# Another recorded order for an attention and two gated layers, with fillers placed by transfers at 1.1 of the model

## The chip, the cores and the metric

The kernel runs on one core of one Trainium2 chip, with TensorE (PE), VectorE (DVE), ScalarE (ACT), GpSimd (POOL) and the transfer queue of SyncE (SP). The metric is the device time of one execution in microseconds; lower is better.

## The reference

Three layers follow each other, for a batch of 4, sequences of 576, 8 heads of 64 and a width of 512. The attention sees a window of 128 positions with a bias by distance; the second layer has a width of 1024 inside.

```
scores = scale * q @ k^T                       # B, H, S, S
scores = where(0 <= rel < 128, scores - slope * rel, -1e9)
x = softmax(scores) @ v                        # laid out as B, S, 512
h = relu(x @ w_in)                             # 512 -> 1024
x = (h * sigmoid(conv3(h))) @ w_out            # 1024 -> 512
x = (sigmoid(conv5(x)) * (x @ w_val)) @ w_out2 # 512 -> 512
```

## The kernel before

Each batch is cut into two halves of the sequence, eight units in all. For a unit the kernel does the attention (`attention` for the first batch, `duo` for the later ones), then `hidden` (w_in, relu, a convolution of 3 taps, the gate), `mixed` (w_out, a convolution of 5 taps), `valued` (w_val times the gate) and `output`. float32 products are made of two rounded halves each: a product of two tiles is three matmuls (L965, L966, L967, or all three at L959 in the later, half-width form). The weights come as float32 in blocks of 128 x 512 into three buffers raw0 to raw2; `widen` (L468 the transfer, L469 and L480 on DVE, L471 on ACT, then a rounding on ACT or POOL, L486 or L487, and a subtraction on POOL, L448) splits each.

In the attention of the first batch a group of blocks passes these steps: scores (PE, L741), the bias and the row's minimum (DVE, L690), the exponential (ACT, L695), the turned-over sum (POOL L699, DVE L701), the scaling (POOL L756, ACT L758 or DVE L762), transposes (PE, L768), an eviction (ACT, L423) and the product with v (PV; PE, L795). Scores and transposes lie in the banks pss0 to pss2, PV in psx0, the dense products in pm0 to pm3. A bank is free for the next product only when the last reader of the one before is done; in `hidden` that is the third multiply-add at L430.

Nothing sets the order at run time. The functions only record operations, with a number each, what they read and write, and the engines that they could run on. `ORDER` is a list of 2,731 entries, a number with a letter: P for PE, A for ACT, D for DVE, G for POOL, S for SP. `Program.order` walks this list, gives each operation that engine, and counts a start for each from a table of durations. Each engine then gets its instructions in the order of the list, and the starts that were counted are used for one more thing: fillers. A filler (L1178) is a small matmul on constants without a use for its result, and the loop at the end of the kernel puts as many as fit into a counted gap of PE:

```
                if fill and o.start < FILL:
                    warm(max(pe, until), o.start)
```

Until 80 us of counted time (`FILL`), a gap gets one for each 160 ns near the start and one for each 125 ns later. `XFER` is a factor on the counted time of each transfer (L160 and after):

```
            if e == "SP":
                dma = max(dma, t + 1100.0) + o.xfer * XFER
                o.end = dma + LAND + o.lat
```

where `o.xfer` is 1.33 times what the recording function gives, 2.85 ns for each of 512 columns for a weight block. So both the list and `XFER` decide how many fillers stand where; the list alone decides the rest.

Of the kernel before, what the change touches and what calls it, by code (L numbers as in the profile page):

```python
# [29 lines left out]
0D 2G 5G 10G 19S 21P 1S 11G 13G 6G 135S 8S 48S 139S 33P 77S 22D 23D 3G 4G 9G 24A 25A 26G 14G 7G 20S 34D 35D 37A 50P  # L30
51D 27D 30G 36A 38G 136D 145S 28A 29P 31P 137A 52D 54A 138D 151S 49S 39D 42D 32A 62P 40G 41P 53A 140D 141A 55G 56D 57G
15G 59A 106S 43P 44A 142D 143G 63D 64D 58P 60P 61A 65A 66A 79P 80D 91P 459S 144G 81D 83A 67G 82A 84G 92D 93D 157S 147A
68D 69G 146D 95A 94A 45P 46A 943D 85D 71G 70P 72P 73A 148D 163S 153A 86G 87P 47D 88G 96G 89P 90A 149G 152D 74P 78S 97D
98A 100G 154D 155A 169S 150G 944D 156G 108P 109D 107S 945D 120P 497S 111A 75A 121D 110D 99P 101P 102A 461P 122D 112A
113G 76D 123A 114D 305P 124A 462D 16G 117G 158D 115A 116P 118P 159A 125G 126D 295P 463D 129G 127G 119A 473P 160D 161G
175S 465A 464A 164D 165A 474D 128P 130P 466G 946D 103P 162G 131A 485P 476A 467D 470G 166D 181S 167G 168G 285P 475D
104A 105D 468A 486D 171A 469P 471P 472A 170D 132P 947D 172D 187S 499P 487A 488G 133A 134D 306P 477A 478G 173A 489D
500D 490G 17G 535S 479D 480G 501D 286P 177A 176D 948D 503A 307A 491P 287A 18G 174G 482G 308A 178D 193S 179G 288A 309D
289D 296P 297A 182D 12G 502A 183A 504G 180G 290D 298A 184D 199S 498S 481P 483P 484A 511P 291A 299D 492A 292D 189A 523P
573S 310D 185G 186G 293A 300D 311A 512D 301A 315P 316P 524D 514A 294G 312D 302D 525A 526G 513D 313A 188D 317A 303G  # L40
336P 337P 515A 314G 505D 190D 205S 319A 326P 327P 506A 516G 338D 195A 508G 507P 509P 194D 304G 318A 320G 527D 528G
517D 339A 196D 211S 520A 340D 328A 191G 529P 510A 537P 321D 460S 341D 329A 200D 322A 323D 518G 342A 530A 192G 519P
330D 201A 343D 324A 331D 197G 202D 217S 521P 522A 344A 325G 332A 538D 203A 206D 198G 207A 346P 347P 539D 541A 348A
333D 561P 549P 550D 807S 356P 204G 208D 540A 212D 349D 209A 223S 562D 494G 542G 543D 213A 210G 357P 358A 563A 546G
551D 350D 359A 493P 536S 367P 368P 214D 229S 334A 360A 351D 345G 495A 218D 219A 361G 564G 496D 215A 220D 235S 335G
352A 544A 553A 216G 552A 554G 531P 574S 949D 224D 545P 547P 225A 532G 353D 381P 362D 548A 575P 221G 555D 558G 226D
241S 363A 950D 222G 354A 355G 556A 557P 559P 227A 228G 565D 364D 230D 231A 382P 395P 560A 952D 576D 232D 247S 566A
587P 951D 533A 365A 577D 236D 233A 567P 366G 588D 237A 534D 234G 589D 568A 578A 579A 238D 253S 383P 242D 243A 239G
240G 369P 599P 1604D 590A 244D 259S 370P 373A 375A 384P 600D 248D 372A 371A 569P 396P 397P 398P 249A 810S 809S 374D
591A 376G 377D 245G 580G 570G 246G 250D 386A 389A 387A 592G 378D 265S 251A 388D 379D 581D 601A 602G 409P 410P 385A  # L50
254D 390G 603D 604G 605P 593D 255A 256D 400A 582A 583P 401A 403A 252G 391D 811S 808S 271S 812S 411P 412P 260D 261A
404G 402D 392D 594A 595P 596A 597P 262D 277S 584A 571A 257G 585P 606A 263G 598A 393D 423P 572D 266D 258G 586A 607P
805S 806S 814S 414A 405D 267A 416D 424P 406D 264G 415A 268D 399A 417A 418G 413A 380A 407D 428P 429P 608G 272D 273A
425D 438P 269A 270G 419D 426A 427G 274D 609A 394A 420D 421D 439P 791S 275A 276G 610D 422A 279A 433P 430D 431A 278D
# [12 lines left out]
705D 1163S 921D 925A 926G 715D 915S 706D 912D 726P 727A 731A 927D 930A 928A 720D 729D 732G 934A 721D 739P 740P 741P
932A 936S 916S 929D 733A 734G 933D 728A 753P 742A 744A 746A 931D 935D 953P 937S 1166S 730D 758P 735D 954D 955P 736D
763P 959D 956D 743A 748A 745D 960D 759P 747G 749G 750D 957D 764P 958G 970G 971D 737A 722A 964A 754P 965D 975G 765D
707A 755D 967A 756A 760D 751D 761G 766G 1192P 1195D 1193D 938P 939A 1197A 757D 762D 941A 767G 1194D 940D 768P 769P  # L70
1199A 752A 942D 976A 781P 1198A 1196D 770D 977D 1171P 1174D 968D 1175D 1167S 1200A 1201G 973A 771A 987G 772G 773P
1178A 1179A 785P 1220S 1172D 1173D 1177A 974D 777P 774P 1176A 1180G 1202D 1209A 984G 778P 1181D 1182A 1184A 775D 988P
989P 1205D 981D 1203D 1188A 1189D 1207A 1211S 1208D 779A 998P 1186A 1221S 1210D 1187D 1206D 978G 990A 786P 991A 1204D
992D 782P 787A 1018P 993D 994A 982G 979G 980D 985A 999P 983D 783A 1019P 986D 1212S 780S 776S 1168G 1169G 1000A 1001A
1008P 1452S 1473S 1183D 995D 1020A 1022A 1002D 1229P 1185D 1003D 1021A 1023G 1009P 1232D 1004A 1230D 1236A 1190S 1472S
1191S 1005D 1029P 1233D 1454S 788S 1170G 1024D 1010A 1011A 1039P 1231D 1025A 1012D 1234A 1030P 1031A 1026D 996G 997G
1013D 1014A 1040P 1453D 1456S 1059P 1060P 1032A 1015D 1049P 1041A 1027G 1028G 1033D 1034D 1006A 784S 1042A 1237A 1043D
1044D 1235A 1007G 1035A 1036D 1468S 1470S 1224S 1223S 1222S 1225S 1238G 1045A 1061A 1217G 1214G 1213P 1215A 1218D
# [101 lines left out]
class Program:  # L180
# [29 lines left out]
    def order(self):  # L210
# [1043 lines left out]
```

## Time and profile before

| | |
|---|---|
| median of 3 runs | 394.82 us (394.79 to 396.17) |
| the profiled execution | 396.73 us, span 394.9 us |
| PE busy | 383.7 us (97%) |
| DVE, ACT, POOL busy | 345.3, 296.0, 241.8 us |
| fillers | 74 |

The span runs from the first to the last instruction. PE is busy nearly throughout, so the table is read as the work of PE and the few places where it has none; the others are busy for 61% to 87% of the span.

### The profile page before, as it was taken

What the parts mean: (1) busy time and instruction counts of PE and PEld (TensorE: products, weight loads), DVE (VectorE), ACT (ScalarE), POOL (GpSimd) and SP (SyncE); (2) the same over time, 40 slices, a digit from 0 to 9 for tenths busy, and PEclk for the clock granted to TensorE, in tenths of its full rate; (3) what the DMA queues carried; (4) which work ended last, traced back from release to release, by engine and by line L of the source; (5) the groups of instructions that cost most, each with busy time, mean ns of one, the idle gap of its engine ahead of it and who ended that gap; (6) DMA issues with size and microseconds to landing.
All of it is one profiled execution on the core that took longest, in us unless ns stands there. A gap on an engine that the chain in (4) does not pass through costs nothing.

```text
span 394.9 us, 10880 instructions
## 1 busy us (share of the span) xinstructions
PE 383.7 (97%) x3878; PEld 335.0 (85%) x3878; DVE 345.3 (87%) x1045; ACT 296.0 (75%) x902; POOL 241.8 (61%) x378
## 2 busy tenths in 40 slices
PE   8899999999999999999999999999999999999996
PEld 7578888899999878998899866799888876898886
DVE  3899999999899999988998999988999898957782
ACT  4889999968796888638887979757986768824561
POOL 2768999958876577825757668460663344741640
PEclk9899999999999999999999999999999999999999
DMA  7967777744646096372762654826455260131001
GB/s 238 314 228 273 239 261 259 238 132 123 170 94 135 11 212 209 71 186 56 185 130 50 195 106 144 165 94 206 106 88 93 77 150 0 26 75 52 0 2 54
DMA packets 64918, 53.77 MB, mean 136 GB/s; under 512 B 44512, under 2 KB 57184, under 8 KB 64864
## 3 DMA queue, kind: packets, MB, share of 16 engines
q1 hardware_dynamic: 64864, 53.08, 49.8%
q8 instruction: 30, 0.49, 0.5%
q14 instruction: 24, 0.20, 0.1%
HBM read 38.51 MB, written 4.72 MB: 109 GB/s over the span
## 4 chain that ended last, share of the span: by engine, by line
PE 53%; DVE 9%; ACT 3%; issue 1%; POOL 0%; DVEq 0%; ACTq 0%
PE pm L959 27%; PE pm L965 7%; PE pm L966 7%; PE pm L967 6%; PE pss L879 3%; PE pss L940 2%; DVE gts L430 2%; DVE t L430 1%; DVE pp L912 1%; DVE hout L610 1%; DVE g L447 1%; DVE gts L1084 1%; ACT pss L695 1%; DVE pss L690 1%; ACT g L1053 0%
## 5 line engine op out<-in xcount | busy, mean ns | idle before, releaser
L959 PE MATMUL pm<-xh,hin 128*128 128x320 f16 (+1 forms) x504 | 68.6, 286 | 0.1
L959 PEld LDWEIGHTS <-hin 128*128 128x128 f16 x504 | 48.0, 97 | 14.2 <-issue 1.1
L959 PEld LDWEIGHTS <-hout 128*128 128x128 f16 x384 | 37.0, 97 | 11.0 <-issue 1.7
L441 POOL TENSOR_TENSOR gts<-gts,t 128x317 f32<-128x317 f32 (+3 forms) x36 | 29.3, 813 | 27.8 <-ACT t L440 11.2
L965 PE MATMUL pm<-g,wout 128*128 128x254 f32 (+3 forms) x128 | 39.7, 310 | 0.3 <-DVE st L701 0.3
L965 PE MATMUL pm<-g,wval 128*128 128x318 f32 (+3 forms) x128 | 39.8, 311 | 0.2
L965 PE MATMUL pm<-g,wo 128*128 128x318 f32 (+3 forms) x128 | 39.2, 306 | 0.0
L690 DVE CUSTOM_DVE_ANT_0 pss<-pss,bm 128x192 f32<-128x192 f32 (+2 forms) x90 | 30.9, 348 | 9.2 <-PE pss L741 7.8
L966 PE MATMUL pm<-g,wo 128*128 128x318 f32 (+3 forms) x128 | 38.1, 298 | 0.3 <-DVE g L447 0.3
L966 PE MATMUL pm<-g,wout 128*128 128x254 f32 (+3 forms) x128 | 38.0, 297 | 0.0
L966 PE MATMUL pm<-g,wval 128*128 128x318 f32 (+3 forms) x128 | 38.0, 297 | 0.0
L967 PE MATMUL pm<-g,wout 128*128 128x254 f32 (+3 forms) x128 | 37.8, 296 | 0.1
L967 PE MATMUL pm<-g,wval 128*128 128x318 f32 (+3 forms) x128 | 37.7, 295 | 0.0
L967 PE MATMUL pm<-g,wo 128*128 128x318 f32 (+3 forms) x128 | 37.7, 294 | 0.0
L1016 ACT ACTIVATE t<-t 128x318 f32<-128x318 f32 (+3 forms) x64 | 28.3, 447 | 10.7 <-DVE t L430 10.1
L695 ACT ACTIVATE pss<-pss,st 128x192 f32<-128x192 f32 (+2 forms) x81 | 30.2, 373 | 6.6 <-DVE st L690 4.8
L430 DVE SCALAR_TENSOR_TENSOR t<-pm,cc,t 128x254 f32<-128x254 f32 (+7 forms) x56 | 28.0, 513 | 2.1 <-ACT t L423 1.2
L430 DVE SCALAR_TENSOR_TENSOR t<-pm,wcc,t 128x318 f32<-128x318 f32 (+3 forms) x56 | 28.2, 512 | 1.3 <-POOL t L441 0.4
L430 DVE SCALAR_TENSOR_TENSOR t<-t,pm 128x318 f32<-128x318 f32 (+3 forms) x64 | 28.4, 448 | 0.9 <-ACT t L1016 0.6
L912 DVE SCALAR_TENSOR_TENSOR pp<-pss,st,pp 128x192 f16<-128x192 f32 (+2 forms) x79 | 28.1, 385 | 1.0 <-ACT pp L908 0.7
L959 PE MATMUL pm<-ghin,hout 128*128 128x318 f16 x192 | 26.8, 298 | 0.2 <-DVE t L430 0.2
L699 POOL TENSOR_SCALAR st<-st 128x4 f32<-128x4 f32 (+3 forms) x44 | 8.8, 199 | 29.6 <-ACT pss L695 11.4
(200 smaller groups left out, 1305.6 us busy)
## 6 DMA issues: line engine op xcount, KB each, us to landing
raw<-in_w_out SPq DMA_DIRECT2D x12, 512.0 KB, 4.0
raw<-in_w_in SPq DMA_DIRECT2D x8, 512.0 KB, 5.1
qkt<-in_qk SPq DMA_DIRECT2D x10, 384.0 KB, 4.5
vr<-in_vN SPq DMA_DIRECT2D x36, 96.0 KB, 3.1
qkt<-in_qk SPq DMA_DIRECT2D x6, 480.0 KB, 4.5
pp<-in_qk SPq DMA_DIRECT2D x6, 480.0 KB, 4.4
raw<-in_vN SPq DMA_DIRECT2D x6, 384.0 KB, 3.8
pp<-in_qk SPq DMA_DIRECT2D x6, 384.0 KB, 3.6
```

Source lines behind the costliest of these rows:

```text
L430: pg.add("DVE", dve_t(n, 0 if isinstance(scalar, float) else 1), lambda: nc.vector.scalar_tensor_tensor(out=out, in0=in0, scalar=scalar, i ...
L441: pg.add("POOL", pool_t(n, True), lambda: nc.gpsimd.tensor_tensor(out=out, in0=out, in1=t, op=ALU.add), prio, (tk,), (key,))
L690: pg.add("DVE", 75 + 1.05 * nkey, lambda: nc.vector.tensor_tensor_reduce(out=s, in0=s, in1=tab[:, 192 - nkey:192], op0=ALU.add, op1=ALU.mi ...
L695: pg.add("ACT", act_t(nkey, True, 2), lambda: nc.scalar.activation(out=to, in_=s, func=AF.Exp, scale=-1.0, bias=best, accum_out=total), pr ...
L699: pg.add("POOL", 165, lambda: nc.gpsimd.tensor_scalar(ri, total, 1e-9, norm, op0=ALU.add, op1=ALU.mult), pr, reads, writes, port=True)
L879: m.append(nc.tensor.matmul(out=s[64 * x:64 * x + 64], lhsT=q_t[y][i][64 * h:64 * h + 64, 64 * h:64 * h + 64], rhs=k_t[y][64 * h:64 * h + ...
L912: pg.add("DVE", dve_t(nkey, 1), lambda sc=sc, hi=hi, lo=lo, ri=ri: nc.vector.scalar_tensor_tensor(out=lo, in0=sc, scalar=ri, in1=hi, op0=A ...
L959: return [nc.tensor.matmul(out=o, lhsT=a, rhs=b_, start=first and i == 0, stop=last and i == 2) for i, (a, b_) in enumerate(((wh, hi), (wh ...
L965: return [nc.tensor.matmul(out=o, lhsT=wh, rhs=hi, start=first, stop=False), nc.tensor.matmul(out=o, lhsT=wh, rhs=lo, start=False, stop=Fa ...
L966: nc.tensor.matmul(out=o, lhsT=wh, rhs=lo, start=False, stop=False),
L967: nc.tensor.matmul(out=o, lhsT=wl, rhs=hi, start=False, stop=last)]
L1016: pg.add("ACT", act_t(Ng), lambda c=c: nc.scalar.activation(out=c, in_=c, func=AF.Tanh, scale=0.5), pr, (), (ak,))
```

## The change

The list is another one: every entry from the first row on may stand elsewhere, and some operations that more than one engine can do have another letter. `XFER` is 1.1 instead of 0.93. Nothing else differs.

```
 ORDER = """
-0D 2G 5G 10G 19S 21P 1S 11G 13G 6G 135S 8S 48S 139S 33P 77S 22D 23D 3G 4G 9G 24A 25A 26G 14G 7G 20S 34D 35D 37A 50P
...
+0D 19S 21P 1S 5G 6G 7G 2G 3G 4G 135S 48S 8S 139S 20S 22D 23D 33P 77S 25A 24A 34D 145S 49S 50P 26G 35D 37A 36A 137A 27D
...
-XFER = 0.93
+XFER = 1.1
```

What the list does is seen in the order of instructions. First TensorE, at the start, in the attention of the first half batch: L741 is a score, L768 a transpose, L795 a PV product (one line further down in the new kernel: L742, L769, L796); L1178 and L1179 are fillers. The old order:

```order
L768 MATMUL pss2_199<-eye_110,pp_192 128x128 x2
...
L741 MATMUL pss1_198<-qkt_177 128x64
L741 MATMUL pss1_198<-qkt_177 128x128
L741 MATMUL pss2_199<-qkt_177 128x192 x2
L795 MATMUL psx0_200<-pp_192,vr_178 64x256 x2
L795 MATMUL psx0_200<-pp_192,vr_178 64x128 x2
L768 MATMUL pss0_197<-eye_110,pp_192 128x128 x4
L768 MATMUL pss1_198<-eye_110,pp_192 128x128 x2
L795 MATMUL psx0_200<-pp_192,v16_179 64x256 x2
L795 MATMUL psx0_200<-pp_192,v16_179 64x128 x2
L741 MATMUL pss0_197<-qkt_177 128x64
L741 MATMUL pss0_197<-qkt_177 128x128
```

One filler stands ahead of these rows and one at the dots. In the new order:

```order
L742 MATMUL pss1_198<-qkt_177 128x128
L769 MATMUL pss2_199<-eye_110,pp_192 128x128
L796 MATMUL psx0_200<-pp_192,vr_178 64x256 x2
L796 MATMUL psx0_200<-pp_192,vr_178 64x128 x2
L742 MATMUL pss2_199<-qkt_177 128x192 x2
L769 MATMUL pss0_197<-eye_110,pp_192 128x128 x4
L742 MATMUL pss0_197<-qkt_177 128x64
L742 MATMUL pss0_197<-qkt_177 128x128
L796 MATMUL psx0_200<-pp_192,v16_179 64x256 x2
L796 MATMUL psx0_200<-pp_192,v16_179 64x128 x2
L769 MATMUL pss1_198<-eye_110,pp_192 128x128 x2
```

The scores on pss2 have moved behind the first PV product, and those on pss0 ahead of the second. Ahead of these rows stand eight fillers, a transpose and two fillers more.

The second place is on VectorE, in the hidden layer of the first half batch, around the last multiply-add on the bank pm1. The old order:

```order
L430 SCALAR_TENSOR_TENSOR t2_134<-pm2_195,cc_109,t2_134 128x254
L430 SCALAR_TENSOR_TENSOR t1_133<-pm1_194,cc_109,t1_133 128x254
L690 ISA pss0_197,st1_191<-pss0_197,bm_113 128x192
L690 ISA st1_191 128x1
L690 ISA pss1_198,st1_191<-pss1_198,bm_113 128x192
...
L430 SCALAR_TENSOR_TENSOR t2_134<-t2_134,pm2_195 128x254
L430 SCALAR_TENSOR_TENSOR t1_133<-t1_133,pm1_194 128x254
```

In the new order the last multiply-add on pm2 is done two rows before the first of these:

```order
L481 SCALAR_TENSOR_TENSOR gts_141<-pm3_196,raw0_114 128x512
L431 SCALAR_TENSOR_TENSOR t1_133<-pm1_194,cc_109,t1_133 128x253
L702 RECIPROCAL st1_191<-st1_191 128x1
L691 ISA pss0_197,st1_191<-pss0_197,bm_113 128x192
L691 ISA st1_191 128x1
L431 SCALAR_TENSOR_TENSOR t1_133<-pm1_194,cc_109,t1_133 128x254
L425 TENSOR_SCALAR t3_135<-pm0_193,cc_109 128x254
L691 ISA pss0_197,st1_191<-pss0_197,bm_113 128x192
L691 ISA st1_191 128x1
L470 TENSOR_SCALAR raw1_115,acc_111<-raw1_115 128x512
L431 SCALAR_TENSOR_TENSOR t1_133<-t1_133,pm1_194 128x254
```

The last one on pm1 has moved behind two steps of the widening of weights (L470, L481), two minima and a first tap on pm0.

Over the whole program TensorE gets 109 fillers instead of 74: 55 instead of 40 up to the products of the fourth PV, and 54 instead of 34 from there to the middle of the first w_out products. DVE has 1,015 instructions instead of 1,022, ACT 762 instead of 760 and POOL 388 instead of 383.

## Rows read from the trace of the kernel before

**Rows 1.** The page's first part: busy time, share, instructions.

```profile
PE 383.7 (97%) x3878; PEld 335.0 (85%) x3878; DVE 345.3 (87%) x1045; ACT 296.0 (75%) x902; POOL 241.8 (61%) x378
```

**Rows 2.** Busy time of each engine by stretch.

```profile
core 0: us, PE busy (x) PEld busy (x) DVE busy (x) ACT busy (x) POOL busy (x), PEclk, DMA share, GB/s
0.00:12.00 12.00, 9.69 (x61) 8.38 (x61) 4.95 (x26) 5.98 (x20) 3.89 (x23) 1.00 0.76 253
12.00:16.00 4.00, 2.88 (x20) 1.95 (x20) 3.32 (x16) 3.50 (x16) 2.87 (x7) 1.00 0.87 263
16.00:20.00 4.00, 3.85 (x18) 2.68 (x17) 2.99 (x10) 2.50 (x6) 3.83 (x7) 0.60 0.95 349
20.00:24.00 4.00, 3.31 (x24) 3.05 (x24) 3.09 (x15) 3.59 (x13) 1.36 (x5) 0.97 0.84 263
24.00:60.00 36.00, 34.22 (x291) 30.39 (x290) 35.25 (x120) 35.23 (x103) 33.97 (x56) 1.00 0.73 251
60.00:380.00 320.00, 318.16 (x3381) 277.50 (x3379) 288.83 (x846) 241.21 (x738) 193.96 (x281) 1.00 0.47 118
380.00:395.00 15.00, 11.63 (x92) 10.99 (x90) 6.90 (x18) 3.97 (x11) 1.89 (x3) 1.00 0.10 35
```

**Rows 3.** The fillers, by their tile: ns least/median/most, first and last start.

```profile
L1178 PE MATMUL psx<-one x74: 245/246/368, 1.1 to 55.5; 128*128 128x192 bf16 x74
```

**Rows 4.** PE's timeline up to 40 us: start, duration, what, wait.

```profile
11.21 0.25 PE L1178 MATMUL psx<-one 128*128 128x192 bf16 x1
...
11.51 0.25 PE L1178 MATMUL psx<-one 128*128 128x192 bf16 x1
...
16.88 1.54 PE L795 MATMUL psx<-pp,v 128*64 128x256 f32 x8
18.36 2.25 PE L741 MATMUL pss<-qkt 128*128 128x64 f32 x8
...
22.35 0.41 PE L965 MATMUL pm<-x,win 128*128 128x256 f32 x1
22.60 0.28 PE L966 MATMUL pm<-x,win 128*128 128x256 f32 x1
...
26.29 0.26 PE L1178 MATMUL psx<-one 128*128 128x192 bf16 x1
...
33.57 1.32 PE L1178 MATMUL psx<-one 128*128 128x192 bf16 x14
```

**Rows 5.** Whom PE waited for, longest in total first.

```profile
PE pss L768 <- POOL pp L756: 2.9, 5, 1.1
...
PE pss L741 <- ACT pp L423: 1.0, 2, 0.7
PE pss L741 <- DMA qkt<-in_qk: 0.5, 1, 0.5
```

**Rows 6.** DVE's timeline at 37 us: pm2's and pm1's last multiply-add.

```profile
36.96 0.76 DVE L430 SCALAR_TENSOR_TENSOR t<-t,pm 128x254 f32<-128x254 f32 x2
```

**Rows 7.** DVE's groups by line, from 24 to 60 us.

```profile
L480 DVE SCALAR_TENSOR_TENSOR gts<-pm,raw 128x512 uint32<-128x512 uint32 x14 | 9.6, 685 | 0.0
L469 DVE TENSOR_SCALAR_CACHE_REDUCE raw<-raw 128x512 uint32<-128x512 uint32 x13 | 8.9, 684 | 0.0
L430 DVE SCALAR_TENSOR_TENSOR t<-pm,cc,t 128x254 f32<-128x254 f32 (+1 forms) x14 | 6.5, 480 | 0.4 <-POOL t L441 0.4
L690 DVE CUSTOM_DVE_ANT_0 pss<-pss,bm 128x192 f32<-128x192 f32 x18 | 6.4, 360 | 0.0
...
L424 DVE TENSOR_SCALAR t<-pm,cc 128x254 f32<-128x254 f32 x1 | 0.5, 480 | 0.0
```

**Rows 8.** PE's timeline from 38 to 50 us.

```profile
38.97 0.28 PE L965 MATMUL pm<-x,win 128*128 128x256 f32 x1
...
40.88 0.82 PE L1178 MATMUL psx<-one 128*128 128x192 bf16 x8
42.39 0.44 PE L768 MATMUL pss<-eye,pp 128*128 128x128 f32 x2 [0.69 <-POOL pp L756]
...
49.91 0.39 PE L965 MATMUL pm<-g,wout 128*128 128x254 f32 x1
```

More of the change, by code (lines that the diff above doesn't have):

```diff
@@ L35 @@
[L35 to L54, printed above, removed]
@@ L160 @@
[L160 to L162 removed]
+0D 19S 21P 1S 5G 6G 7G 2G 3G 4G 135S 48S 8S 139S 20S 22D 23D 33P 77S 25A 24A 34D 145S 49S 50P 26G 35D 37A 36A 137A 27D
+28D 30D 51D 29P 31P 32A 38G 14G 136D 52D 138D 39D 42D 53A 62P 140D 54A 40G 106S 63D 141A 41P 43P 55G 56D 64D 151S 57G
@@ new lines @@
+1031A 1032D 1059P 1060P 1027G 1028G 1454S 1231D 1014A 1015D 1225S 1033D 1049P 1224S 1041A 1042A 1043D 1006G 1007G
+1061A 1063A 1034D 1471S 1223S 1222S 1213P 1016G 1044D 1035A 1214G 1062D 1217G 1045A 1036D 1050P 1064G 1215A 1046D
+1218A 1453D 1070P 1017G 1084P 1047G 1048G 1216D 1219D 1236A 1051A 1052A 1053D 1071P 1234A 1037A 1038G 1235A 1065D
+1237A 1238G 1054D 1066A 1275G 1055A 1250P 1538S 1239D 1242A 1085P 1067D 1112P 1456S 1056D 1244A 1243D 1068A 1057G
+1251D 1255A 1098P 1086P 1058G 1253D 1254D 1240A 1257A 1226G 1258A 1246A 1252D 1256A 1455D 1072P 1069D 1087P 1227A
@@ new lines @@
+1259G 1260D 1267A 1241D 1272G 1228G 1475S 1245D 1261A 1268D 1073P 1262D 1089A 1457D 1265A 1621G 1088A 1263A 1078A
+1090A 1269S 1247D 1264D 1099P 1113P 1076A 1266D 1091D 1458P 1075A 1077D 1459D 1079G 1080D 1100P 1092A 1093G 1114P
+1081D 1270S 1460A 1074A 1461P 1465D 1101P 1094D 1082D 1115P 1104A 1541S 1477S 1249S 1248S 1537S 1095D 1096D 1106A
+1627G 1126P 1117A 1102A 1119D 1131P 1103A 1105D 1127P 1120A 1107G 1108D 1118A 1121G 1463D 1097A 1083A 1116A 1473S
+1539S 1132P 1109D 1464D 1110D 1136P 1474S 1467G 1122D 1111A 1133D 1128D 1540S 1536S 1271P 1123D 1124D 1476S 1134A
@@ new lines @@
+1561A 1290A 1157S 1530S 1543S 1502D 1508S 1159P 1282D 1503D 1283D 1298P 1557A 1291A 1160A 1292D 1293D 1299P 1559A
+1284A 1285D 1294A 1300D 1542S 1545S 1286G 1295D 1308P 1309P 1560A 1558A 1509S 1556A 1562G 1329P 1821S 1301D 1302D
+1303D 1287G 1563D 1330P 1310A 1311A 1312A 1296G 1319P 1320P 1304A 1331D 1313G 1572A 1305D 1332A 1333D 1306G 1314D
+1339P 1340P 1321A 1546G 1297G 1322A 1334D 1315A 1323D 1531P 1335A 1307G 1316D 1570A 1336D 1324D 1317G 1349P 1341A
+1342A 1573D 1318G 1568A 1343D 1344D 1374P 1534A 1532A 1350P 1535D 1564A 1325A 1547G 1548G 1375P 1533D 1566D 1345A
@@ new lines @@
+1326D 1327G 1565D 1578P 1351A 1337A 1346D 1161S 1352A 1338G 1360P 1581D 1347A 1825S 1579D 1580D 1388P 1353A 1354G
+1574D 1576S 1575D 1584A 1361P 1328G 1571D 1355D 1583A 1585A 1389P 1348G 1582D 1356A 1357D 1362P 1376P 1586A 1569D
+1820S 1824S 1358A 1587G 1588D 1567D 1577S 1595D 1589A 1593A 1390P 1822S 1823S 1359G 1363P 1391P 1591A 1364A 1377P
+1366A 1368A 1369G 1596D 1592D 1590D 1594D 1598S 1613P 1392A 1396A 1402P 1403P 1365D 1367D 1378A 1380A 1382A 1614D
+1615P 1383G 1379A 1394A 1397G 1370D 1371D 1616D 1617D 1404P 1405P 1393A 1372D 1381D 1384D 1416P 1618G 1385D 1398D
@@ new lines @@
+1826G 1622G 1406A 1408A 1386D 1850P 1625A 1410A 1387A 1597S 1599P 1399D 1395D 1619G 1411G 1400D 1407A 1409D 1421P
+1827A 1620G 1645G 1412D 1417P 1602A 1413D 1828G 1373A 1603D 1600A 1418D 1419A 1420G 1422P 1426P 1601D 1829P 2126S
+1853D 1857A 1880S 1882S 1414D 1431P 1423D 1401A 1623D 1424A 1425D 1415A 1628A 1427P 1851D 1855A 1633G 1634G 1878S
+1879S 1631A 1854D 1832D 1432P 2127S 2131S 1428D 1833D 1429A 1430G 1837A 1830D 1440P 1436P 1433D 1434A 1852D 1856A
+1831D 1448P 1858A 1435D 1437P 1629D 1635D 1834A 1441P 1835A 1836A 1449P 1438A 1859G 1442A 1838G 1883S 1860D 1867A
@@ L163 @@
+2723P 2715P 2694A 2712D 2713G 2714D 2709D 2724P 2727P 2720P 2725D 2726S 2721A 2722S 2716P 2728P 2717A 2718S 2729A
+2730S
 """
```

217 lines of the change are left out of this document (105 added, 112 removed).

## The prediction, before the result was known

> **What bounds the kernel now.** I read the share of busy time first, then the busy time by stretch, then who TensorE (PE) waited for, and only then single places of the timeline. PE is busy for 383.7 us of a span of 394.9 us [rows 1], and its matmuls are the same in both kernels but for the fillers, so the time is the sum of that work and of whatever PE loses. The table by stretch shows where it loses [rows 2]. From 60 to 380 us PE is idle for only 1.84 us. At the end it is idle for 3.37 of 15 us, behind its last product. The first 60 us hold the rest: 2.31, 1.12, 0.15, 0.69 and 1.78 us, 6.05 us together. Fillers count as busy: there are 74, all between 1.1 and 55.5 us [rows 3]. Fourteen in a row took 1.32 us, 0.094 us each [rows 4]; 74 at that price are 7.0 us. So PE does about 13 us of nothing useful in the first 60 us, and under 2 us from there to the end of its work. What is to be won or lost stands mainly in the first 60 us.
>
> Which engine sets the pace there? From 24 to 60 us VectorE (DVE) is busy for 35.25 and ScalarE (ACT) for 35.23 of 36 us [rows 2]. Before 24 us no engine is full: the chain from a transfer over scores, minimum, exponential, scaling and transposes runs step by step. PE's waits say the same: 2.9 us for GpSimd's (POOL) scaling L756, 1.0 us for ACT's eviction L423, 0.5 us for a transfer [rows 5].
>
> **The change part by part.** The diff replaces the list of 2,731 places and one constant. No operation is added but fillers: 74 become 109. Counted in the order of instructions, DVE has 1,015 instead of 1,022, POOL 388 instead of 383, ACT 762 instead of 760. The sum is made against the profiled execution, whose span of 394.9 us stands in a run of 396.73 us, 1.9 us over the median of 394.82; I apply the difference to the median.
>
> *The early chain.* In the new order the score matmuls on pss0 stand ahead of the second PV product instead of behind it; those on pss2 stand behind the first PV product instead of ahead. The second PV product took 1.54 us at 16.88 us, with the scores behind it [rows 4]. DVE, which takes the minimum of these scores, is busy for 2.99 of 4 us from 16 to 20 us and for 3.09 from 20 to 24 [rows 2]: 1.92 us that it could use. Bounds: nothing (the chain waits for POOL anyway) and -1.5 us. The pair that moves back takes part of it; I take -0.9 us.
>
> *The clock.* The granted clock averages 0.60 from 16 to 20 us and 0.97 in the next four [rows 2]: some 3.4 us at 1.2 GHz, work that takes 1.7 us at 2.4 GHz. Ahead of it PE idled for 1.12 of 4 us, and between the fillers at 11.51 and 26.29 us the old order has none [rows 4]. The new one has ten where those at 11.21 and 11.51 stood, then none until behind the first product of the hidden layer, where it has seven. So only the start of that stretch is better filled. Bounds: 0 and -1.7 us; PE is not the only step of the chain there, and I take -0.5 us. The Trainium skill, "TensorE: Matmul & The Clock Gate", Part 1, says that the array is slow by default, that activity releases it, and that the place where it does so varies from run to run; by that this term would be 0 or -1.7 us in one and the same kernel. The trace agrees in so far as the slow spell follows an idle stretch; no row here shows whether it moves between runs.
>
> *The fillers.* 35 more at 0.094 us are 3.3 us of PE time. Fifteen of them stand ahead of the end of the fourth PV product (55 instead of 40), where PE has most of its idle time: 2.31 + 1.12 + 0.15 + 0.69 us up to 24 us. Twenty stand later, where it has 1.78 us [rows 2]. The factor on transfers matters here: with 1.1 the program counts 512 x 2.85 x 1.33 x 1.1 = 2.13 us for a weight block of 512 KB, 246 GB/s; with 0.93 it is 1.80 us and 291 GB/s. The queue moved 349 GB/s when its engines were 0.95 busy and 263 at 0.87 and 0.84 [rows 2], so 1.1 is on the slow side, and some of the gaps that it fills are not there. On the other hand the fillers at 0.93 left 6 us of idle time. A filler in a real gap costs nothing, and one elsewhere costs 0.094 us. Bounds: 0 and +3.3 us. I let a little over a quarter of them be paid: +0.9 us.
>
> *Late releases.* In the hidden layer of the first half batch, DVE's last multiply-add on bank pm1 frees it for a later product. Before, it stood right behind the one on pm2; the two took 0.76 us from 36.96 us [rows 6]. Now there lie from one to the other an L480, an L424, an L469, two L690 and three L430, the last included: 0.69 + 0.48 + 0.68 + 2 x 0.36 + 3 x 0.48 = 4.0 us by their rows [rows 7]. That is 3.6 us more than the 0.38 of one multiply-add. The next product on pm1 started at 38.97 us [rows 8], 1.25 us after the release at 37.72; with eight fillers ahead of it now (0.75 us) it can wait for up to 3.6 - 1.25 - 0.75 = 1.6 us. It is partly a swap: before, PE spent 0.82 us on eight fillers and 0.69 us in a wait from 40.88 to 42.39 us [rows 8]. Bounds 0 and +1.6 us; I take +0.6 us.
>
> *Changes of kind on PE.* The first dense product behind a score took 0.41 us, the one behind it 0.28 [rows 4]. Scores, transposes and PV products of the first batch are entered from another kind 35 times instead of 38, the products on quarters of the array in the later batches 30 times instead of 31: 4 x 0.13 = 0.5 us. I take -0.4 us, with 0 as the other end.
>
> *After 60 us.* DVE has seven instructions less, of about 0.5 us (L424 has 0.48 [rows 7]): 3.5 us; POOL has five more. From 60 to 380 us DVE is busy for 289 of 320 us and POOL for 194 [rows 2], so work leaves the fuller engine. PE's idle time of 1.84 us is all that can be won; a new order can lose as much or more at other places. I take -0.6 us, between -1.8 and +2.0. The end keeps its form (last product, ACT's eviction, the transfer out): 0.
>
> Sum: -0.9 - 0.5 + 0.9 + 0.6 - 0.4 - 0.6 = -0.9 us, from 394.8 to **393.9 us**. A measurement of this kernel can tell about 0.5% (2 us) from no change, so the forecast is a change too small to tell, on the side of a gain.
>
> **The rivals.**
> *Faster (391.9 us).* The gaps are real, so the fillers are free and the late release only takes the place of the wait at 42 us. The early chain and the clock give together all of DVE's idle time from 16 to 24 us: -1.9 - 0.4 - 0.6 = -2.9 us. For it speaks that before 24 us DVE is idle for 24 - 14.35 = 9.65 us [rows 2], so there is something to win. Against it: from 24 to 60 us DVE and ACT are full with nearly the same work, which only an earlier start makes end earlier.
> *Slower (397.4 us).* The fillers are paid: transfers land as fast as before, PE's next product is ready, and the 20 fillers from the fourth PV product to the w_out products, with five of those at the start, run ahead of it. 25 x 0.094 = 2.35, with +0.6 for the release and -0.4 for the kinds: +2.6 us. It decides once 19 of the 35 run while the next real matmul is ready (1.8 + 0.2 us). For it speaks the transfer rate above; against it the 6 us of idle time that PE had beside 74 fillers.
> *The change does not do what it says.* The loss of the first 60 us is set by DVE's and ACT's work, and only moves from idle time to fillers: 394.8 us, no change to be told, like the forecast.
>
> **How the numbers follow.** The forecast with the third rival, 393 to 396.7 us: 0.43. Faster: 0.37, since 13 us are lost in the first 60 us and more of the terms point that way. Slower: 0.20. So faster by over 0.5% 0.37, within 0.5% 0.43, slower by over 0.5% 0.20. The forecast's own range is 393.0 to 396.0. The 8-in-10 range reaches into both rivals: down to 390.8, where all of the 1.84 us after 60 us is won too, and up to 397.6 us.
>
> **What would show it.** The early chain: the first product of the hidden layer starts before 22.35 us [rows 4], and DVE is busy for over 6.5 of the 8 us from 16 to 24 us. The clock: no stretch before 24 us under 0.9. The fillers: PE's idle time of the first 60 us falls below 4 us, with 109 fillers. Late releases: a wait of PE for DVE near 39 us. After 60 us: PE idle for under 2 us up to 380 us. The prediction is wrong if PE's waits after 60 us exceed 4 us (a poorer order later), or if the first w_out product starts over 2 us away from 49.91 us [rows 8].

## The result and the profile after

The changed kernel takes **390.6 us** (median of 4 runs, 390.36 to 391.05) where the kernel before, on the same chip, takes 394.81 (4 runs, 393.69 to 396.17): a ratio of 0.987 [0.984, 0.990]. The forecast was 393.9 us and its range began at 390.8, so the gain of 4.2 us is more than four times the 0.9 us that were forecast. It is the side of the faster rival (391.9), and goes past that too. The profiled execution took 390.36 us, its span is 388.4 us. PE is busy for 381.8 us (98%), DVE for 338.0 (7.3 less than before), ACT for 298.1 (2.1 more). There are 109 fillers instead of 74, from 1.1 to 63.5 us.

Busy time by stretch of the changed kernel, to be held against [rows 2]:

```profile
0.00:12.00 12.00, 10.33 (x74) 8.95 (x76) 5.59 (x32) 6.56 (x22) 3.73 (x21) 1.00 0.82 266
12.00:16.00 4.00, 3.23 (x24) 2.16 (x22) 3.79 (x18) 3.32 (x13) 2.85 (x7) 1.00 0.97 294
16.00:20.00 4.00, 3.94 (x33) 3.03 (x30) 3.89 (x17) 3.66 (x11) 3.36 (x6) 1.00 0.90 296
20.00:24.00 4.00, 3.76 (x32) 3.19 (x30) 3.80 (x15) 3.65 (x14) 3.31 (x8) 1.00 0.97 325
24.00:60.00 36.00, 35.47 (x309) 31.67 (x306) 35.35 (x116) 35.58 (x106) 33.90 (x53) 1.00 0.80 262
60.00:380.00 320.00, 319.82 (x3418) 281.63 (x3415) 284.35 (x845) 244.23 (x741) 195.63 (x291) 1.00 0.48 115
380.00:388.00 8.00, 5.23 (x44) 5.02 (x42) 1.19 (x3) 1.16 (x3) 0.41 (x1) 0.97 0.19 66
```

PE's idle time of the first 60 us is 1.67 + 0.77 + 0.06 + 0.24 + 0.53 = 3.27 us (before 6.05), and from 60 to 380 us 0.18 us (before 1.84). Fillers count as busy, and the 35 additional ones are 3.3 us at the 0.094 us of [rows 4], so the fall in the first 60 us alone says nothing about time won. DVE is full from 12 us on, where before it had 1.92 us left between 16 and 24. No stretch has a lower clock before the end. The waits of PE (for whom, us in total, times, longest) from 0.2 us up are four; the 2.9 us for GpSimd's scaling [rows 5] are no longer among them:

```profile
PE psx L1179 <- DVE one L1106: 1.1, 1, 1.1
PE pss L742 <- ACT pp L424: 1.0, 2, 0.8
PE pss L742 <- DMA qkt<-in_qk: 0.5, 1, 0.5
PE psx L796 <- DVE x L675: 0.2, 1, 0.2
```

PE's timeline at the places of [rows 4] and [rows 8]:

```profile
14.88 0.71 PE L742 MATMUL pss<-qkt 128*128 128x64 f32 x4 [0.76 <-ACT pp L424]
15.60 0.87 PE L796 MATMUL psx<-pp,v 128*64 128x256 f32 x8
...
18.31 0.41 PE L966 MATMUL pm<-x,win 128*128 128x256 f32 x1
...
36.82 0.59 PE L1179 MATMUL psx<-one 128*128 128x192 bf16 x5
37.24 0.38 PE L769 MATMUL pss<-eye,pp 128*128 128x128 f32 x2
37.46 0.41 PE L1179 MATMUL psx<-one 128*128 128x192 bf16 x3
37.94 0.39 PE L966 MATMUL pm<-x,win 128*128 128x256 f32 x1
...
48.21 0.36 PE L966 MATMUL pm<-g,wout 128*128 128x254 f32 x1
```

The scores now run ahead of the PV product, which takes 0.87 instead of 1.54 us; the hidden layer begins at 18.31 instead of 22.35 us, w_out at 48.21 instead of 49.91. Part of this is the clock and not the order. A second profile of the kernel before (e13 below) holds no stretch at 1.2 GHz, and there the same places read:

```profile
16.74 0.87 PE L795 MATMUL psx<-pp,v 128*64 128x256 f32 x8
...
20.65 0.41 PE L965 MATMUL pm<-x,win 128*128 128x256 f32 x1
...
48.19 0.38 PE L965 MATMUL pm<-g,wout 128*128 128x254 f32 x1
```

So the PV product takes 0.87 us in the old order too, the new one begins the hidden layer 2.3 us earlier, and at the first w_out product nothing of this lead is left.

The product at 37.94 us follows eight fillers without a wait. But the step of DVE that frees pm1 for it ends only at 37.88 us, and e15, the same list without these fillers, has the wait:

```profile
37.47 0.41 DVE L431 SCALAR_TENSOR_TENSOR t<-t,pm 128x254 f32<-128x254 f32 x1
```

```profile
37.16 0.39 PE L960 MATMUL pm<-x,win 128*128 128x256 f32 x1 [0.73 <-DVE t L425]
```

Both kernels do the same 3,804 matmuls besides the fillers, so the time at which the n-th of them starts can be compared wherever the stages lie. Counted from 0 in the matmul records, in us:

| | 400th | 800th | last | 800th to last |
|---|---|---|---|---|
| before, profile of [rows 1] | 68.06 | 109.77 | 391.52 | 281.75 |
| before, a second profile (e13) | 66.39 | 108.10 | 389.66 | 281.56 |
| changed | 65.29 | 106.44 | 384.95 | 278.51 |
| changed, a second profile (e12) | 64.95 | 106.33 | 385.45 | 279.12 |

The first profile of before holds 3.41 us at 1.2 GHz (the expectations below call this the spell) and the second none: its 800th product comes 1.67 us earlier. Between the second and the changed kernel lie 4.7 us: 1.1 up to the 400th product, 0.6 up to the 800th and **3.05 behind it**, in the part where PE's idle time before was 1.84 us.

### The profile page after: what moved, and what is told of

It reads as the page before. It is cut to its first block, busy times and chain, and to the rows that moved or that the text cites. A ratio compares the mean times of both kernels' runs of the same rounds, so it can differ in the third digit from the quotient of the medians.

```text
span 388.4 us, 10935 instructions
## 1 busy us (share of the span) xinstructions
PE 381.8 (98%) x3913; PEld 335.6 (86%) x3913; DVE 338.0 (87%) x1038; ACT 298.1 (77%) x904; POOL 243.2 (63%) x383
## 4 chain that ended last, share of the span: by engine, by line
PE 53%; ACT 0%; issue 0%
PE pm L960 27%; PE pm L966 7%; PE pm L967 7%; PE pm L968 6%; PE pss L880 3%; PE pss L941 2%; ACT t L424 0%; PE psx L941 0%; PE pss L624 0%; PE psx L880 0%; ACT pp L909 0%; PE pss L573 0%; PE pss L632 0%; PE psx L579 0%
## 5 line engine op out<-in xcount | busy, mean ns | idle before, releaser
L960 PE MATMUL pm<-xh,hin 128*128 128x320 f16 (+1 forms) x504 | 68.1, 286 | 0.0
L960 PEld LDWEIGHTS <-hin 128*128 128x128 f16 x504 | 48.3, 97 | 13.6 <-issue 0.5
L960 PEld LDWEIGHTS <-hout 128*128 128x128 f16 x384 | 37.2, 98 | 10.2 <-issue 0.8
L700 POOL TENSOR_SCALAR st<-st 128x4 f32<-128x4 f32 (+3 forms) x44 | 8.6, 195 | 36.6 <-ACT pss L696 19.9
L1007 ACT ACTIVATE pm<-pm,wsc 128x320 f32<-128x320 f32 (+1 forms) x42 | 19.9, 476 | 9.8 <-PE pm L960 9.4
```

Source lines behind the costliest of these rows:

```text
L960: return [nc.tensor.matmul(out=o, lhsT=a, rhs=b_, start=first and i == 0, stop=last and i == 2) for i, (a, b_) in enumerate(((wh, hi), (wh ...
L1007: pg.add("ACT", act_t(Nx, True, 1 if half else 0) + 35, lambda h=h: nc.scalar.activation(out=h[:, 0:Nx], in_=h[:, 0:Nx], func=AF.Relu, sca ...
```

## The experiments

The theory at the start: half of the gain is one swap at the start (scores on pss0, entry 108, ahead of the second PV product, entry 74), the other half the order after 60 us, and the constant with its fillers is worth nothing. The rivals: the fillers hold PE's clock, or the order of the first 60 us is the whole gain. In the files of the experiments lines stand 5 lower than in the kernel before (L736 a score, L763 a transpose, L790 PV, L954 and L960 dense products, L1173 a filler); e12 and e13 are the two kernels themselves. ORDER below is `new` or `old`; `join(a, n, b)` stands for the first n + 1 entries of a and then what is missing, in b's order.

**Which part of the list, and the constant (e1 to e4).**

```
e1  ORDER = join(new, place of 423, old); XFER = 1.1     # 423: first w_val product, about 62 us
e2  ORDER = join(old, place of 423, new); XFER = 0.93
e3  ORDER = new; XFER = 0.93
e4  ORDER = old; XFER = 1.1
```

> The new list up to the first product with w_val (about 62 us), then the old list's order for all that is left; the factor on transfers is 1.1, so the fillers of the first 60 us are those of the new kernel. If the gain is made in the first 60 us (early chain, clock) and only carried along, this is as fast as the new kernel: about 390.6 us. If a good part of it is made after 60 us, where PE's many short pauses became fewer, it loses that part: the traces put 2.4 us of 6.5 us before 62 us, so about 392.5 to 393.5 us. If the late part alone counts: 394.8 us.

> The old list up to the first product with w_val, then the new list's order; factor 0.93, so the old fillers. The counterpart: 394.8 us if the gain is all early, 392 to 393 us if two thirds of it are made after 60 us, 390.6 us if all of it is late.

> The new list with the factor of transfers at 0.93: 69 fillers instead of 109, nothing else changed. If the fillers are free because the gaps are real (faster rival): 390.6 us, unless the clock falls without them, which would cost up to 1.7 us (392.3 us) and show a granted clock of 0.6 in some stretch before 24 us. If fillers were paid at 0.094 us each: 386.8 us; at the quarter that the prediction took: 389.6 us.

> The old list with the factor at 1.1: 127 fillers instead of 74. If more fillers keep the clock up and are free: 393.1 to 394.8 us, and no slow spell at 16 to 20 us. If they are paid: up to 5.0 us more, 399.8 us; at a quarter, 396.0 us.

| | us (runs) | ratio to before |
|---|---|---|
| e1 new, then old | 396.13 (12) | 1.001 [0.999, 1.003] |
| e2 old, then new | 393.67 (11) | 0.995 [0.993, 0.997] |
| e3 new list, 0.93 | 390.85 (5) | 0.987 [0.984, 0.989] |
| e4 old list, 1.1 | 397.76 (11) | 1.005 [1.002, 1.007] |

e1 lies above all that I expected of it, e2 between two of its cases (it has 82 fillers, not the old 74), e3 where fillers are free and e4 where they are paid. The list is the whole gain: with 69 fillers instead of 109 (e3) it is as fast, and on the old list 127 fillers cost (e4). The early part alone shows nothing in time (e1), but its join is at fault too: PE waits once for 2.0 us there, the longest wait in its list, so the lists were joined elsewhere next.

```profile
PE psx L790 <- ACT pp L418: 2.0, 1, 2.0
```

**A join where the lists nearly meet (e5, e6, e16).** At entry 802, about 105 us, the first parts differ in three operations only.

```
e5, e16  ORDER = join(new, 802, old); XFER = 1.1
e6       ORDER = join(old, 802, new); XFER = 0.93
```

> The cut of the first two runs moved to a place where both lists have done nearly the same work: entry 802, about 105 us, where three operations differ. New list first, then the old one's order; factor 1.1. In the traces the new kernel is 3.3 us ahead at this place. If the 2.0 us wait of the first run was a matter of the seam, no such wait is here, and the time is 391.5 to 392.5 us: ahead by 3.3 us against a before with the slow spell, without the 3 us that the new order gains later. If the early gain can't be kept by the old order, 394.8 us or more.

> Old list up to entry 802, then the new one's order; factor 0.93. If the gain after 105 us belongs to the new order itself: 392 to 393.5 us, with about half of the executions some 1.5 us slower by the slow clock spell at 16 to 20 us, as in before. If it rests on the lead that the early part gives: 394.8 us.

> The new list up to entry 802 and the old one behind it, once more. Theory A (the head is the changed kernel's, and only the first profiled execution had late transfers): the 800th product at 106.2 to 106.9 us in the profile, the stretch behind it 282.2 to 282.8 us, the time 393.9 to 394.6 us. Rival B (the head pays only with the new tail): the 800th product at 107.5 us or later again, the time 394.9 us or above.

e5: 395.1 us (10), 0.998 [0.996, 1.000]; e16, the same kernel: 394.7 (12), 0.998 [0.996, 1.000]; e6: 393.23 (5), 0.992 [0.989, 0.996]. e6 came out in its first case (the gain after 105 us belongs to the new order), e5 in its last. From the 800th product to the last e5 took 282.43 and e16 282.67 us, e6 278.47. So the late part of the new list is worth some 3 us whatever stands ahead of it: in the eight profiles that have it (e2, e3, e6, e8, e11, e12, e15 and the changed kernel's) it takes 278.5 to 279.2 us, in the seven with the old late part unaltered (e1, e4, e5, e9, e13, e16 and [rows 1]) 281.6 to 282.8. The early part is harder to price: the 800th product came at 108.39 and 107.47 us with the new head, the first part of the new list (106.44 in the changed kernel), so neither e16's theory nor its rival came out. PE's instructions up to the join are the changed kernel's; in e5 512 KB blocks of w_in took 6.1 us to land where the changed kernel's took 4.8 (medians). A joined list also loses at its join: behind the 600th product e16 took 302.7 us, the kernel before 301.1 and 300.9.

**The engines of the list, and the swap (e7, e8, e9).**

```
e7   ORDER = new, each entry with old's engine letter (181 differ)
e8   -... 93D 108P 94A 95A 148D 163S 47D 74P 86A 109D ...
     +... 93D 94A 95A 148D 163S 47D 74P 108P 86A 109D ...
e9   -... 152D 74P 78S 97D 98A 100G 154D 155A 169S 150G 944D 156G 108P 109D ...   # the old list
     +... 152D 108P 74P 78S 97D 98A 100G 154D 155A 169S 150G 944D 156G 109D ...
```

> The new list's order with the old list's engines: 181 operations go back to the engine that they had (DVE has its seven instructions more again, POOL its five less). If the relief of DVE makes the gain after 60 us, it goes: about 393.5 to 394 us, with short waits of PE for DVE all along. If the order alone makes it: 390.6 to 391.5 us. As the order was made for the new engines, some single waits of up to 1 us are expected in either case.

> The new kernel with one entry moved: the score pair on pss0 goes back behind the second PV product, as in the old order. If that swap makes part of the early gain, as the prediction held (0.9 us), the time is 391.0 to 392 us, DVE idles more from 16 to 20 us, and the clock may fall there again. If it is of no account: 390.6 us.

> The old list and the old constant, with one entry moved: the scores of 108P stand directly ahead of the second weighted sum 74P instead of eleven entries behind it (two more fillers follow from the new gaps). Theory A (this one swap is most of what the first 25 us gain, and it ends the 1.2 GHz spell because TensorE has the scores to do while it would stand idle): 1.0 to 2.2 us under the kernel before in the executions without a spell, no 1.2 GHz record before 60 us, so 392.9 to 394.2. Rival B (the swap only pays among its new neighbours; alone it moves the wait to the next weighted sum): within 0.5 us of before, spell still in some executions.

e7: 416.7 us (4), 1.051 [1.047, 1.056], far beyond both cases that I expected; one of the four executions took 758.1 us, and no profile of that one is kept. The new order with the old engines makes PE wait for DVE's evictions all through the program, so places and engines belong together:

```profile
PE pm L954 <- DVE t L425: 6.5, 10, 1.3
PE pss L874 <- DVE xh L676: 2.3, 4, 0.9
PE pm L954 <- ACT t L418: 2.2, 2, 1.4
```

e8: 392.78 us (4), 0.991 [0.987, 0.994], 2.1 above the changed kernel, which ran on another chip; in the profiles its 800th product comes at 107.91 us, 1.5 later. With the scores behind the PV product PE stands still ahead of it, where the scores had run:

```profile
13.39 0.84 PE L763 MATMUL pss<-eye,pp 128*128 128x128 f32 x4
15.75 0.87 PE L790 MATMUL psx<-pp,v 128*64 128x256 f32 x8 [1.52 <-ACT pp L690]
16.55 0.71 PE L736 MATMUL pss<-qkt 128*128 128x64 f32 x4
```

But e9, the same swap in the old list, gains nothing: 396.47 us (12), 1.002 [1.000, 1.004], and its profile holds the 1.2 GHz stretch at the same place as before. (It has 72 fillers, two fewer than before and not two more; e8 has 114.) The swap is worth 1.5 to 2.1 us among its new neighbours and nothing alone; theory A of e9 failed.

**The fillers (e11, e12, e15).**

```
-FILL = 80000.0
+FILL = 0.0        # e11: no fillers; e15: 9000.0, the first 33 (20 ahead of the first scores, then 8, 1, 4)
```

> The new list with no fillers at all. Theory A (on the new list fillers neither cost nor buy: no stretch of TensorE's queue is empty long enough for the clock to fall): 390.2 to 391.0 us, no 1.2 GHz record before 60 us. Rival B (the fillers hold the clock in the first 60 us): records of 1.2 GHz there of 3 us or more, 1.5 us or more beyond the new kernel in the same call, 392 or above.

> The changed kernel once more, beside the three others, for the spread of its own executions. Theory A (the new list leaves no place for the spell): every execution within 0.8 us, 390.3 to 391.1, mean clock 0.998 or more. Rival B (the spell is luck of few executions): some executions 1.4 us longer at a mean clock near 0.995.

> The new list with only the 33 fillers that stand ahead of 9 us (20 ahead of the first scores, then 8, 1 and 4). Theory A (the 4 us that no fillers cost are the first scores at half rate, and fillers behind 9 us buy nothing on this list): 390.4 to 391.2 us, as with all 109. Rival B (fillers between 9 and 60 us hold the rate too): a stretch of scores or products at twice their usual time behind 9 us, 392 us or above.

e12, the changed kernel again: 390.7 us (6), 0.989 [0.986, 0.992]. e11: 394.71 (12), 0.998 [0.996, 1.000]; e15: 390.14 (6), 0.987 [0.984, 0.991]. The first 33 fillers are worth 4 us (394.71 against 390.7), the other 76 nothing. What they buy is seen at the first scores, of e11:

```profile
3.91 2.50 PE L736 MATMUL pss<-qkt 128*128 128x64 f32 x8 [3.91 <-DMA qkt<-in_qk]
6.84 1.22 PE L736 MATMUL pss<-qkt 128*128 128x64 f32 x4 [0.42 <-DMA qkt<-in_qk]
7.86 0.64 PE L763 MATMUL pss<-eye,pp 128*128 128x128 f32 x2
8.97 1.65 PE L736 MATMUL pss<-qkt 128*128 128x192 f32 x4 [0.47 <-ACT pp L418]
```

and of e15:

```profile
4.23 1.30 PE L736 MATMUL pss<-qkt 128*128 128x64 f32 x8
...
6.35 0.71 PE L736 MATMUL pss<-qkt 128*128 128x64 f32 x4 [0.16 <-DMA qkt<-in_qk]
...
7.33 0.48 PE L763 MATMUL pss<-eye,pp 128*128 128x128 f32 x2 [0.18 <-issue]
...
8.28 0.92 PE L736 MATMUL pss<-qkt 128*128 128x192 f32 x4
```

The same groups take 1.3 to 1.9 times as long in e11. This goes on up to 16 us: the next PV product takes 1.55 us, in e15 0.87, and the transposes at 16.22 us are back at the 0.60 that e15 has at 9.03.

```profile
13.53 1.55 PE L790 MATMUL psx<-pp,vr 128*64 128x256 f32 x8
...
16.22 0.60 PE L763 MATMUL pss<-eye,pp 128*128 128x128 f32 x4
```

```profile
11.09 0.87 PE L790 MATMUL psx<-pp,vr 128*64 128x256 f32 x8
```

The trace's first entry for the clock, at 2.4 GHz, begins at 15.98 us in e11 and at 4.25 us in e15, and ahead of it there is no entry at all: the 1.00 that the table by stretch prints there is the lack of an entry, not a reading. So the first 33 fillers bring the rise of PE's clock forward by some 12 us. Theory A of e11 failed; rival B has the right time (over 392 us), though the slow part lies ahead of the first entry and not in a record of 1.2 GHz. e12 fits neither of its theories: no execution has the lower clock, but two of the six took 391.9 and 392.2 us. e15 came out just under theory A: behind 9 us it leaves PE idle for 3.66 us between 24 and 60 us, and loses nothing.

**The kernel before again (e13).**

> The kernel before once more, for its profile. Theory A (most of the 4 us are behind 105 us, the early part is worth 1 to 2 us): without a 1.2 GHz record the 800th product comes at 107.3 to 108.5 us, and the stretch from there to the last product takes 281.7 to 282.8 us. Rival B (the early part is worth nothing without the spell): the 800th product at 106.4 us or before, as in the changed kernel.

395.24 us (8), 1.000 [0.997, 1.002]. Its profile has no 1.2 GHz stretch, and theory A holds but for 0.14 us: the 800th product at 108.10 us, 281.56 us behind it. Busy time by stretch:

```profile
12.00:16.00 4.00, 2.93 (x20) 1.88 (x20) 3.33 (x16) 3.46 (x15) 2.89 (x7) 1.00 0.81 265
16.00:20.00 4.00, 3.19 (x23) 2.30 (x22) 3.97 (x15) 3.61 (x10) 3.83 (x7) 1.00 0.96 317
20.00:24.00 4.00, 3.97 (x28) 3.58 (x30) 3.55 (x17) 3.79 (x15) 2.83 (x9) 1.00 0.83 284
```

PE idles for 1.07 of 4 us from 12 to 16 us, as in [rows 2] (1.12), and the clock stays at 2.4 GHz. DVE, whose idle time from 16 to 24 us I had taken for the room of the early chain, is busy for 7.52 of these 8 us: most of that room was the 1.2 GHz stretch itself.

**Where the late gain comes from (e10, e14, e17, e18).** Most of the late part's 3 us is not in PE's idle time, which behind the 800th product is 1.06 us in e13 and 0.18 in the changed kernel: matmul records overlap. A place of e13:

```profile
347.22 0.30 PE L965 MATMUL pm<-g,wo 128*128 128x318 f32 x1
347.86 0.41 PE L966 MATMUL pm<-g,wo 128*128 128x318 f32 x1 [0.34 <-DVE g L447]
```

These records last 0.30 us and usually follow each other at 0.147. So of the 0.64 us from the first to the second 0.50 are lost; the profile calls 0.34 of it a wait, and a loss of up to 0.15 us is not seen as idle at all. I summed, for the dense products behind the 800th, what each distance to the next start has above the usual one of its shape, where that is over 60 ns. Old late parts: 8.9 to 11.0 us in 11 profiles (before 9.3, e13 9.0). New ones: 6.4 to 7.2 in 8 (changed 6.5, e12 7.1). So 2 to 3 of the 3.05 us are such pauses. The six longest that I could mend in the old list came from an operation that frees a bank or feeds a product and stands in its queue behind an unrelated one. I moved those ahead (e10), then four of them (e14); or gave 15 operations between 125 and 200 us from DVE to ACT, as the new list does (e17), and moved three besides (e18).

```
e10  775D ahead of 1181D, 1148D of 1484D, 1152D of 1487D, 1673D of 1692D, 2503G of 2544G; 2111D 2114S behind 1702D
e14  without 1673D and 2111D 2114S
e17  old list, letter A for 775 1205 1218 1246 1261 1265 1134 1152 1498 1496 1291 1310 1572 1321 1534
e18  e17, and 775A ahead of 1209A, 1148D of 1484D, 2503G of 2544G
```

> The old list and constant, with six small moves after 105 us, none on TensorE: at six of the longest pauses of TensorE's stream the operation that it waits for is taken out from behind an unrelated one (775 ahead of 1181, 1148 ahead of 1484, 1152 ahead of 1487, 1673 ahead of 1692, 2111 with its transfer 2114 behind 1702, GpSimd's 2503 ahead of 2544). The pauses are 0.23, 0.30, 0.38, 0.29, 0.35 and 0.50 us beyond the usual spacing, 2.05 us in all, of 3.3 us that the new list gains from the 800th product to the last. Theory A (the tail's gain is made of such pauses, each an operation that frees a bank or feeds a product and is queued behind another): 279.7 to 280.4 us from the 800th product to the last, where the kernel before takes 281.75; time 1.3 to 2.0 us under before. Rival B (the pauses only wait further on: the next product waits for the operation that was passed over): 281.3 to 282 us, time as before within 0.5.

> The old list with four of the six moves (775, 1148, 1152 and 2503; 1673, 1692, 2111 and 2114 stand as before). In the run with six, the stretch from the 800th product to the last was 0.14 us under that of the old list with the swap: 1.24 won by 187 us, 0.82 of it given back at 197 us, 0.79 lost at 240 to 245 us, 0.52 won at 349 us. Theory A (a pause taken away stays won unless another engine is the limit behind it): 0.9 us under the 282.8 us of the old tail in the same records, so 281.7 to 282.1; time 0.5 to 1.0 under before in the executions without a spell. Rival B (all is given back): 282.6 to 282.9.

> The old list with 15 operations between 125 and 200 us given from the vector engine to the scalar engine, all of them ones that the new list gives over too (775, 1152 and 13 others, some 6 us of work); order as before. Theory A (the vector engine's load sets the pace there): the stretch from the 800th to the 1800th product takes 91.6 to 92.2 us, where the kernel before took 92.8 and 92.5, the changed one 91.7; time 0.4 to 1.0 us under before in the executions without a spell. Rival B (the operations stand in the scalar engine's queue at places where they wait behind its own): 92.5 us or more, with new waits of TensorE for the scalar engine, and no gain in time.

> As e17, and three moves: 775, now the scalar engine's, directly ahead of 1209; 1148 ahead of 1484; GpSimd's 2503 ahead of 2544. Theory A (with the vector engine relieved, pauses that are taken away stay away): the stretch from the 800th product to the last takes 280.2 to 281.0 us, where the kernel before took 281.75 and 281.56 and the list with four moves 282.4; time 0.9 to 1.5 us under before in the executions without a spell. Rival B (given back again): 281.5 us or more, no gain in time.

| | us (runs) | ratio to before | 800th to last, us | pauses, us |
|---|---|---|---|---|
| e10 | 396.51 (12) | 1.002 [0.999, 1.004] | 282.64 | 9.7 |
| e14 | 395.07 (12) | 0.998 [0.996, 1.000] | 282.44 | 9.9 |
| e17 | 398.46 (11) | 1.007 [1.005, 1.010] | 285.35 | 11.0 |
| e18 | 398.07 (12) | 1.007 [1.004, 1.009] | 284.89 | 10.0 |

Theory A failed each time. e17 and e18 came out as rival B has it, e10 worse than that (282.64 us), and e14 between the two (282.44 us; without the stretch at 1.2 GHz 394.84 us against 395.28, 0.4 under before). From the 800th to the 1800th product e17 took 96.4 us, where theory A had 91.6 to 92.2. In e14 the pause at 347 us became shorter (GpSimd's 2503 moved: DVE's subtraction took 1.16 us instead of 1.66), and others came. PE came to the products at 195.57 us earlier (196.41 in e9, the old late part), and stood there for the bank:

```profile
195.57 1.49 PE L954 MATMUL pm<-xh,hin 128*128 128x260 f16 x12
197.56 1.16 PE L954 MATMUL pm<-xh,hin 128*128 128x260 f16 x9 [0.51 <-DVE t L425]
```

DVE's timeline of e14 up to that release, in which it never idles:

```profile
195.43 0.49 DVE L1003 TENSOR_SCALAR pm<-pm,wsc 128x260 f32<-128x260 f32 x1
195.83 1.35 DVE L425 SCALAR_TENSOR_TENSOR t<-pm,cc,t 128x257 f32<-128x257 f32 x3
197.09 0.41 DVE L425 SCALAR_TENSOR_TENSOR t<-t,pm 128x258 f32<-128x258 f32 x1
197.43 0.87 DVE L425 SCALAR_TENSOR_TENSOR t<-pm,cc,t 128x257 f32<-128x257 f32 x2
```

Taking work off DVE at unchanged places in the list made it worse, with waits for both engines (e17, 125 to 205 us):

```profile
PE pm L954 <- DVE t L425: 1.9, 2, 1.0
PE pm L954 <- ACT t L418: 0.8, 1, 0.8
```

## Why the prediction was wrong, step by step

- **After 60 us: the step that failed.** It said that "PE's idle time of 1.84 us is all that can be won" there and took -0.6 us. Idle time was the wrong measure: the records overlap, so PE loses more than the profile calls idle. Measured: -0.6 us from the 400th to the 800th product (-0.3 to the second profile) and -3.05 (-2.4) behind, of which 0.9 is idle time and 2 to 3 us, idle or not, are pauses. The bound of -1.8 us was passed, and the range's lower end hung on it; by its own terms that end is 391.9 - (1.84 - 0.6) = 390.7 us, not 390.8. That the gain is in pauses is shown; that DVE's 4.5 us less from 60 to 380 us made it is not, since no part of the new list that I tried brought it alone.
- **The early chain** came near in size, partly by luck: -0.9 us taken. The two rows that it was read from, the 1.54 us of the PV product and DVE's idle time, were the stretch at 1.2 GHz, which the next term counted again: in e13 they are 0.87 us and 0.48 instead of 1.92. The hidden layer does start 2.3 us earlier than in e13, but at the first w_out product the lead is gone (48.21 against 48.19 us). The new head is ahead by 1.1 to 1.4 us at the 400th product against e13, and by 0.6 to 1.0 against e6, whose head is the old one (65.93 us; e13 lost more to a transfer, a wait of 1.5 us for qkt where e6 has 0.6 and the changed kernel 0.5). That is made behind 48 us, and no run tells by what. The swap that I named is needed (e8), but does nothing alone (e9).
- **The clock** at -0.5 us was about right as a mean. Of 121 executions of the kernel before beside the experiments, 40 have a mean granted clock of 0.996 or less, and there the medians are 1.4 to 2.1 us longer. Of 75 with the new head, in whatever experiment, 3 have it. The Trainium skill's statement that the place of the rise varies from run to run ("TensorE: Matmul & The Clock Gate", Part 1) agrees with the traces: in one program the first entry at 2.4 GHz begins at 6.55 us (the profile of [rows 1]) and at 4.29 us (e13), and the first of these has the stretch and the second not. The 2.3 us between them are more than the ±500 ns that the Trainium skill gives there. Where the stretch shows, it lies from 16.5 or 17.0 to 19.9 or 20.4 us, in all eight profiles that hold it.
- **The fillers** at +0.9 us: 0 in the end (e3, e15). On the way they do cost: without the 76 later ones the first w_out product starts at 46.82 us (e15) instead of 48.21, and by the 400th product (64.86 against 65.29) most of that is gone. The paid ones are on the old list: 53 more cost 1.4 to 2 us (e4: 397.76 against 395.79, or 396.44 against 395.09 without the 1.2 GHz stretch).
- **Late releases** at +0.6 us: the mechanism is there, covered by fillers. The release comes at 37.88 us and the product at 37.94; PE spends the time before on eight fillers, and without them waits 0.73 us for this step (e15). As with the fillers, it does not show in the whole time. The wait of 0.69 us at 42 us is gone; eleven fillers stand there (40.33 us), where e15 waits 0.66 us for ACT.
- **Kinds** at -0.4 us: not told apart.
- **The sum:** -1.1 - 0.6 - 3.05 = -4.7 us against e13's profile, whose span of 393.1 us stands 4.7 above 388.4. The signs to look for came out (18.31 us, 7.69 of 8 us of DVE, 3.27 us of idle time, no lower clock, 48.21 us) but for the wait near 39 us, which fillers hide. They were weak signs: the unchanged kernel passes three of them in e13 (20.65 us, 7.52 of 8 us, no lower clock), the idle time falls by the fillers themselves, they would have fitted the faster rival as well, and the late gain was not among them.

What stays open: which of the new list's places behind 105 us bring the 3 us. Moving six operations, moving four, giving fifteen to another engine, and that with three moves brought no gain clear of the spread, so the late order as a whole is shown to be the cause, and no step of it.

## What to carry to other kernels

Where an engine's records overlap, its idle time is not what it loses: sum the distances from start to start beyond the usual one. A pause is not always a price that can be collected at its place: here, where DVE never idled ahead of the next bank (e14), it only moved on; so an order is tested as a whole, and a list that is cut and joined loses at the join. Before fillers are costed, find which of them work: here the first 33 do, and the other 76 neither cost nor bring anything on the new list. A filler also hides a wait: look for waits in a run without fillers. And compare a profile with a second one of the same kernel before a row is priced: here two rows of the first were a stretch at 1.2 GHz that most executions don't have.

## What the runs showed of the hardware

- Without work ahead of the first scores PE runs at half rate for long: in e11 (no fillers) up to 15.98 us, where the trace's first entry for the clock begins; with 33 fillers from 1.06 us on (e15) up to 4.25 us. Ahead of the first entry the printed clock of 1.00 is no reading; the lengths of the groups tell the rate.
- The rise falls at different places in executions of one program. The same eight scores behind the same 18 fillers, in the profile of [rows 1] (first entry at 6.55 us) and in e13's (4.29 us):

```profile
3.91 2.39 PE L741 MATMUL pss<-qkt 128*128 128x64 f32 x8
```

```profile
3.91 1.48 PE L741 MATMUL pss<-qkt 128*128 128x64 f32 x8
```

- The 1.2 GHz stretch comes and goes between executions of one program, with the same 1.1 us of idle time ahead of it (e13 and [rows 2]). With the old head it goes along with the rise: the eight profiles that hold it have the first entry at 6.2 to 6.7 us, the two without (e13, e6) at 4.29 and 5.23. With the new head none of ten profiles holds it, with first entries from 4.1 to 6.9 us and at 15.98 (e11). No run moves the rise alone, so that it decides is not shown.
- DVE's subtraction of two SBUF tiles at L447 took 1.66 us while GpSimd's L847 ran, and ended 0.34 us behind it; others of its shape that run beside no GpSimd instruction take 0.47 to 0.49 us. In e13:

```profile
346.14 1.66 DVE L447 TENSOR_TENSOR g<-gts,g 128x318 fp32r<-128x318 f32 x1 [0.54 <-ACT g L413]
```

```profile
345.80 1.66 POOL L847 TENSOR_TENSOR v<-vr,v 128x768 f16<-128x768 f32 x1
```
